# One TensorE visit for states @ w1, attention's small tiles gathered into two slots of three, and batch 0's states doubled on the chip

## The chip, the cores and the metric

The kernel runs on one core of a Trainium2 chip. The time is the device time of one execution in microseconds; before the change it was 436.61 us, the median of three runs (436.3 to 436.9). The profile is one execution of 436.56 us, of which 434.8 us lie between the first and the last instruction; its TensorE clock was granted in full. PE is TensorE, DVE is VectorE, ACT is ScalarE, POOL is GpSimd, SP is the engine that issues most transfers.

## What is computed

Two stages follow each other: a cross attention between tokens and states of each batch and head, and a layer of eight experts in which every row goes to the expert with the largest gate.

```python
# x: (8, 8, 512, 64), state: (8, 8, 32, 64), all fp32
scores = 0.125 * x @ state.T            # per batch b and head h
a      = softmax(scores);   xread = a @ state      # 512 rows
scores2 = 0.125 * state @ x.T
a2     = softmax(scores2);  sread = a2 @ x         # 32 rows
rows   = concat([xread, sread]) -> (8 * 544, 512)  # heads side by side
e      = argmax(rows @ w_gate);  g = max of softmax
out    = g * (relu(rows @ w1[e]) @ w2[e])          # w1: (8, 512, 1024), w2: (8, 1024, 512)
```

The kernel uses two properties of this. All 512 token rows of a batch mostly go to one expert, so a batch is a dense product with that expert's weights; the few others would be repaired behind a branch, which isn't taken with these inputs. And since xread = a @ state, the product xread @ w1 can be taken as a @ (state @ w1): the kernel first forms G = state @ w1 for the batch, from 32 rows per head, and then multiplies the attention weights by G. The 256 state rows are sorted by expert and done in rounds of 128 rows between the batches.

## The kernel before

Work is written as Python generators. `down` and `up` issue the large products of the experts, and after every four large matmul instructions, a "slot", they call `next(insert)`, which issues a step of other work: first the attention of later batches (each batch is a generator `stages(b)`; a new one begins every third slot), then the rounds of the state rows. In the order below the steps of a batch are one slot apart.

```python
def load_states(b, q0, q1):
    rows = state[b].rearrange("h n d -> n h d")
    to = st2[b] = att.tile([64, H, D], FP32, tag="st", bufs=3, name="st2")
    q0.dma_start(out=to[0:32], in_=rows)
    for u in range(2):                     # the same states, halves exchanged
        q1.dma_start(out=to[32:64, :, ts(u, 32)], in_=rows[:, :, ts(1 - u, 32)])

def turn_states(b, copy):                  # stT: transposed by DVE, then copied to the other 64 partitions
    ...
    dve.transpose(to[0:64], st2[b][:].rearrange("p h d -> p (h d)"))
    copy(to[64:128], to[0:64])
    for g in range(2):
        gp.tensor_copy(out=stG[ts(g, 64), b], in_=...)

def stages(b):
    xt, sx = new_xt(b), new_sx()
    for k in range(2):
        turn_x(b, xt, k)                   # DVE: x transposed
    turn_states(b, gp.tensor_copy)
    yield
    states_gates(b)                        # PE pg   64*32 tiles
    pc = new_pc()
    scores(b, xt, pc, 0)                   # PE pc   32*32 tiles
    yield
    scores(b, xt, pc, 1)                   # PE pc
    for i in range(4):
        turn_scores(pc, sx, i)             # DVE sx <- pc
    less_max(sx, ALL, gp)                  # DVE mx, POOL sx
    nm = write_max(pc)                     # DVE nm
    yield
    soft[b] = (sx,) + write_weights(pc, nm)   # ACT a
    exponential(sx, ALL)                   # ACT sx
    over_sum(sx, ALL, gp)                  # DVE sm, POOL sx
    yield
    turn_read(b)                           # DVE aT
    yield
    turn_write(b)                          # PE pt   whole array
    yield
    write_rows(b)                          # PE pw   128*32 tiles
    exps, gates = logits_x(b)              # PE pl   128*32 tiles, then DVE routing
    yield
    exps()
    xsT = turn_rows(b)                     # PE pxs  whole array
    yield
    choose(b)                              # PE pr   whole array
    logits_s(b, [xsT])                     # PE pls  128*32 tiles, DVE lgs
    gates()

def states_w1(G, w1t, st, halves=(0, 1), bank=bank, cut=1):
    for k in halves:
        pg = [bank("pG") for _ in range(2)]
        for q in range(4):
            for g in range(2):             # PE pG  64*32 tiles
                pe.matmul(pg[g][ts(q, 32), :], lhsT=st[ts(g, 64), q, :],
                          rhs=w1t[ts(g, 64), q, ts(k, 512)], start=True, stop=True, ...)
        for c in range(cut):
            for g in range(2):
                act.copy(G[:, g, ...], pg[g][...])
    return G

def between_products(n):                   # after the n-th product pX, pD, pX, pY, pZ, pW of batches 2 to 7
    nonlocal G
    if n in (3, 4) and b + 1 < B:          # one half of G in each of two slots
        if n == 3:
            G = new_G()
        states_w1(G, w1s[b + 1], stG[:, b + 1], (n - 3,), <banks of a second pool>)
    yield
    if n == 4 and b + 2 < B:
        lazy.extend(w1_parts(b + 2, expert_of(eb, b + 2)))
    if n == 5 and b + 1 < B:
        sums_of[b + 1] = up_sums(G, aT[b + 1])
    yield
```

All PSUM tiles that `bank()` gives (pg, pt, pw, pl, pls, pr, pxs, pG, py, ph) share four buffers of one bank each. [...] A matmul of fp32 stands in the profile as two records.

Of the kernel before, what the change touches and what calls it, by code (L numbers as in the profile page):

```python
# [9 lines left out]
FP32 = mybir.dt.float32  # L10
# [10 lines left out]
def kernel(  # L21
# [76 lines left out]

    st2 = {}

    def load_states(b, q0, q1):

        rows = state[b].rearrange("h n d -> n h d")
        to = st2[b] = att.tile([64, H, D], FP32, tag="st", bufs=3, name="st2")
        q0.dma_start(out=to[0:32], in_=rows)
        for u in range(2):
            q1.dma_start(out=to[32:64, :, ts(u, 32)], in_=rows[:, :, ts(1 - u, 32)])

    wg = const.tile([128, NDC, E], FP32)
    wg4 = att.tile([128, NDC, 32], FP32, name="wg4")  # L110
    act.dma_start(out=wg4[:, :, 0:E], in_=moe_w_gate.rearrange("(p c) e -> p c e", c=NDC))
    load_states(0, sp, act)
    load_x(0, sp)
    dve.memset(wg4[:, :, E:], 0.0)
    warm = const.tile([128, 1], FP32)
# [74 lines left out]
    blank = ffn.tile([128, XW], I32, tag="y", bufs=YB, name="blank")  # L190
    gp.memset(blank[:], 0)
    gp.memset(blank[:, DM + 1:DM + 2], FAR)
    gp.memset(gst[:], 0.0)

    soft, rows_of = {}, {}
# [12 lines left out]
    def turn_states(b, copy):  # L208

        stT[b] = att.tile([128, H, 2, NS], FP32, tag="stT", bufs=2, name="stT")  # L210
        to = stT[b][:].rearrange("p h u n -> p (h u n)")
# [3 lines that stand above are left out]
            gp.tensor_copy(out=stG[ts(g, 64), b], in_=stT[b][:].rearrange("p (q g) u n -> p g u q n", g=2)[ts(g, 64), g, 0])  # L215
# [61 lines left out]
    def new_xt(b):  # L277

        return [(att, ffn)[b % 2].tile([128, 4, NC, 2, 32], FP32, tag=("xt0", "xt1", "Sa", "Sb")[2 * (b % 2) + k], name="xt")
                for k in range(2)]  # L280

    def new_sx():
        return att.tile([128, 4, NB, NS], FP32, tag="sx", bufs=2, name="sx")
# [35 lines left out]
    def fetch_batch(b):  # L319
        if b < B:  # L320
            load_x(b, sp)
            load_states(b, sp, sp)

    def turn_read(b, i=ALL):
        if b not in aT:
            aT[b] = att.tile([128, 4, 2, 128], FP32, tag="aT", bufs=NE, name="aTe")[:]
        dve.transpose(aT[b][:, i].rearrange("p i g s -> p (i g s)"),
                      soft[b][0][:, i].rearrange("p i b n -> p (i b n)"))
        if i.stop == 4 and b != 1:
            keep_read(b)  # L330
# [14 lines left out]
    def stages(b):  # L345

        xt, sx = new_xt(b), new_sx()
        for k in range(2):
            turn_x(b, xt, k)
        turn_states(b, gp.tensor_copy)  # L350
        yield
        states_gates(b)
        pc = new_pc()
        scores(b, xt, pc, 0)
        yield
        scores(b, xt, pc, 1)
        for i in range(4):
            turn_scores(pc, sx, i)
        less_max(sx, ALL, gp)
        nm = write_max(pc)  # L360
        yield
        soft[b] = (sx,) + write_weights(pc, nm)
        exponential(sx, ALL)
        over_sum(sx, ALL, gp)
        yield
        turn_read(b)
        yield
        turn_write(b)
        yield
        write_rows(b)  # L370
        exps, gates = logits_x(b)
        yield
        exps()
        xsT = turn_rows(b)
        yield
        choose(b)
        logits_s(b, [xsT])
        gates()

    def turn_rows(b):  # L380

# [42 lines left out]
    def choose(b):  # L424

        most(b, count(b))
# [17 lines left out]
    def begin():  # L444
# [17 lines left out]
        most(0, pr)  # L462
        keep_warm(6)
        xt, sx = new_xt(0), new_sx()
        turn_x(0, xt, 0)
        turn_states(0, act.copy)
        e = expert_of(eb, 0)
        at_once(w1_parts(0, e, 2))
        load_x(1, sp)
        load_states(1, sp, sp)  # L470
        sp.dma_start(out=wg[:], in_=moe_w_gate.rearrange("(c p) e -> p c e", p=128))
        at_once(w2_parts(0, e))
        fetch_batch(2)
# [33 lines left out]
        up(G, aT[0], hT, two, fs=far)  # L507
        nm = write_max(pc)
        xt, sx = new_xt(1), new_sx()
        for k in range(2):  # L510
            turn_x(1, xt, k)
        turn_states(1, gp.tensor_copy)
        first_e = att.tile([1, 1], FP32, name="first_e")
        dve.tensor_copy(out=first_e[:], in_=eb[0:1, 0:1])

# [71 lines left out]
    def new_G():  # L587
        return ffn.tile([128, 2, F], FP32, tag="G", name="G")

    def states_w1(G, w1t, st, halves=(0, 1), bank=bank, cut=1):  # L590

        for k in halves:
            pg = [bank("pG") for _ in range(2)]
# [3 lines that stand above are left out]
                              rhs=w1t[ts(g, 64), q, ts(k, 512)], start=True, stop=True, skip_group_check=True)  # L597
            for c in range(cut):
                for g in range(2):
                    act.copy(G[:, g, ts(cut * k + c, 512 // cut)], pg[g][:, ts(c, 512 // cut)])  # L600
        return G

    def new_hT():
# [107 lines left out]
        next(insert, None)  # L711
        return hT

    def down(hT, w2t, store, insert=None, between=None):
        for c in range(NC):
            py = bank("py")
            for f in range(NFC):
                pe.matmul(py[:], lhsT=hT[f // 2][:, f % 2, ts(c, 128)], rhs=w2t[:, f, :],
                          start=(f == 0), stop=(f == NFC - 1))
                if insert and f == 3:  # L720
                    next(insert, None)
            store(c, py)
            if insert:
                step = between(c)
                next(step)
                next(insert, None)
                next(step)
# [340 lines left out]
    def first():  # L1068

        write_rows(0)  # L1070
        keep_read(1)
        yield
        turn_write(1)
        yield
        exps, gates = logits_x(1)
        yield
        exps()
        choose(1)
        e1 = expert_of(eb, 1)
        at_once(w1_parts(1, e1))  # L1080
        lazy.extend(w2_parts(1, e1))
        gates()
        count(0)
        yield
        write_rows(1)
        yield
        xsT = [turn_rows(b) for b in range(2)]
        yield
        logits_s(0, xsT)
# [8 lines left out]
    def attention():  # L1098

        gens, slot = [first()], 0  # L1100
        while gens:
            b = 2 + slot // 3
            old, new = gens[:], slot % 3 == 0 and b < B
            begun = slot < 6
            if slot == 2:
                early.append(stages(3))
                next(early[0])
            if begun:
                advance(gens, old[:1])
            if new:  # L1110
                if not early:
                    early.append(stages(b))
                    next(early[0])
                gens.append(early.pop())
            advance(gens, old[1:] if begun else old)
            slot += 1
            yield

# [8 lines left out]
    def batch(b):  # L1127

        nonlocal G, hT

        def between(c):
            nonlocal G
            if c == 1 and b:
                G = states_w1(new_G(), w1s[b + 1], stG[:, b + 1])
            yield
            if c == 2 and not b:
                G = states_w1(new_G(), w1s[b + 1], stG[:, b + 1])
            if c == 1 and 0 < b < B - 2:
                lazy.extend(w1_parts(b + 2, expert_of(eb, b + 2)))
            yield  # L1140

        def between_products(n):
            nonlocal G
            if n in (3, 4) and b + 1 < B:
                if n == 3:
                    G = new_G()
                states_w1(G, w1s[b + 1], stG[:, b + 1], (n - 3,),
                          lambda name: late["ps_t"].tile([128, 512], FP32, tag="t", bufs=2, name=name))
            yield
            if n == 4 and b + 2 < B:  # L1150
                lazy.extend(w1_parts(b + 2, expert_of(eb, b + 2)))
            if n == 5 and b + 1 < B:
                sums_of[b + 1] = up_sums(G, aT[b + 1])
            yield

        if b < NE:
            down(hT, w2s[b], store_batch(b), slots, between)
        else:
            last = down_by_halves(b, hT, w2s[b], slots, between_products)
        if 0 < b < B - 2:  # L1160
            lazy.extend(w2_parts(b + 2, expert_of(eb, b + 2)))
        if b + 1 in sums_of:
            hT = up_by_halves(G, aT[b + 1], sums_of[b + 1], new_hT(), slots)
        elif b + 1 < B:
            hT = up(G, aT[b + 1], new_hT(), insert=slots, at=(1, 3, 5, 7) if b + 1 < NE else (1, 3, 4, 5, 6, 7))
        if b == B - 1:
            return last
        if b == 0:
            e2 = expert_of(eb, 2)
            lazy.extend(w1_parts(2, e2) + w2_parts(2, e2))  # L1170
# [130 lines left out]
```

## Time and profile before

| | busy, us | share of the 434.8 us span | instructions |
|---|---|---|---|
| PE | 425.4 | 98% | 3925 |
| PE weight loads | 287.9 | 66% | 3925 |
| DVE | 220.6 | 51% | 475 |
| POOL | 153.7 | 35% | 144 |
| ACT | 128.9 | 30% | 297 |

| part of the work, all batches | records | busy, us |
|---|---|---|
| pG (states @ w1), 64*32 tiles | 256 | 17.1 |
| pc (scores), 32*32 tiles | 1024 | 19.1 |
| pw (a2 @ x), 128*32 tiles | 512 | 8.9 |
| pl, pls (gates of rows), 128*32 tiles | 192 | 8.2 |
| pg (gates of states), 64*32 tiles | 128 | 2.5 |
| pt, pxs (transposes), whole array | 72 | 10.8 |

A group is named "out<-in" by the tiles that it writes and reads; "128*32" is the part of the array that one matmul takes, in rows and columns, and "x32" the number of records. In a timeline the columns are the start, the time from the first start to the last end, the engine, the line (48, the recording helper, for nearly all), the operation, the tiles, the shape and, in brackets, how long the engine was idle before and for whom it waited. Matmuls overlap, so what one of them costs the stream is read from the difference of two starts. 110 MB are moved by DMA at a mean of 253 GB/s.

### The profile page before, as it was taken

To read this page: it belongs to the slowest core of one execution; us is meant where nothing else is said; L and a number is where in the kernel's file an instruction comes from. 1 tells how busy PE (TensorE), PEld (TensorE's weight loads), DVE (VectorE), ACT (ScalarE), POOL (GpSimd) and SP (SyncE) were. 2 spreads that over 40 slices of the span, in tenths; PEclk is the share of its full clock that TensorE was granted. 3 is DMA by queue.
4 is the path that set the end of the run, shared out by engine and by line. 5 is a ranking of instruction groups with operands and counts; after the bars stand their busy time and mean duration, and the time that the engine had idled before them with its cause. 6 is when DMAs were issued, how large, how long until landed. Compare 5 with 4: busy or idle time off the path is not lost.

```text
span 434.8 us, 10177 instructions
## 1 busy us (share of the span) xinstructions
PE 425.4 (98%) x3925; PEld 287.9 (66%) x3925; DVE 220.6 (51%) x475; ACT 128.9 (30%) x297; POOL 153.7 (35%) x144
## 2 busy tenths in 40 slices
PE   6899999999999999999999999999999999999996
PEld 5686555555545558786668667776867685768665
DVE  5658967587686557333415261624442370527142
ACT  1455133552452532212321241013240242015100
POOL 2010231223222512473427424634336253644231
PEclk9999999999999999999999999999999999999999
DMA  7990659664685454899999699689948998975212
GB/s 218 319 326 4 190 176 328 200 217 134 201 310 171 134 201 133 309 349 404 386 390 354 200 331 392 258 281 396 384 150 236 402 386 279 311 247 214 97 35 74
DMA packets 64899, 110.06 MB, mean 253 GB/s; under 512 B 13327, under 2 KB 22799, under 8 KB 64848
## 3 DMA queue, kind: packets, MB, share of 16 engines
q1 hardware_dynamic: 60240, 99.99, 66.6%
q0 software_dynamic: 2240, 7.08, 4.3%
q10 hardware_dynamic: 2368, 2.31, 1.5%
q8 instruction: 32, 0.52, 0.5%
q14 instruction: 19, 0.16, 0.1%
HBM read 94.15 MB, written 14.95 MB: 251 GB/s over the span
## 4 chain that ended last, share of the span: by engine, by line
PE 94%; DVE 2%; DMA 1%; ACT 0%; issue 0%; ACTq 0%; POOL 0%; DVEq 0%
PE ph L48 23%; PE py L48 13%; PE pX L48 10%; PE pD L48 8%; PE pY L48 5%; PE pZ L48 5%; PE pgy L48 5%; PE pgh L48 5%; PE pW L48 5%; PE pc L48 4%; PE pG L48 3%; PE pw L48 2%; PE pt L48 2%; PE pE L48 2%; DMA st<-in_state_dram 1%; PE pl L48 1%
## 5 line engine op out<-in xcount | busy, mean ns | idle before, releaser
L48 PE MATMUL py<-w2t,hT 128*128 128x512 f32 x128 | 59.1, 604 | 0.0
L48 DVE TENSOR_TENSOR hT<-ph,hT 128x512 f32<-128x512 f32 x50 | 34.6, 692 | 40.7 <-PE ph L48 40.7
L48 POOL TENSOR_TENSOR Ta<-w2t,Ta 128x1024 f32<-128x1024 f32 x12 | 30.6, 2546 | 46.6 <-PE pY L48 19.9
L48 PE MATMUL pX<-w2t,hT 128*128 128x256 f32 x192 | 43.7, 381 | 0.0
L48 PEld LDWEIGHTS pX<-w2t,hT 128*128 128x128 f32 x192 | 36.2, 190 | 6.4 <-issue 1.7
L48 PEld LDWEIGHTS py<-w2t,hT 128*128 128x128 f32 x128 | 23.0, 189 | 26.3 <-issue 25.3
L48 ACT ACTIVATE hT<-ph 128x512 f32<-128x512 f32 (+2 forms) x50 | 22.7, 462 | 40.2 <-PE ph L48 40.2
L48 PE MATMUL ph<-aTl,G 128*128 128x256 f32 (+1 forms) x112 | 33.8, 444 | 0.0
L48 PE MATMUL ph<-aTe,G 128*128 128x128 f32 (+2 forms) x128 | 30.4, 388 | 1.6 <-DVE aTe L48 1.4
L48 DVE SCALAR_TENSOR_TENSOR yh<-pY,gw,yh 128x256 f32<-128x256 f32 x22 | 9.2, 477 | 44.3 <-PE pY L48 37.7
L48 ACT ACTIVATE yh<-pX,gw 128x256 f32<-128x256 f32 x34 | 13.7, 474 | 52.6 <-PE pX L48 52.6
L48 POOL DMA_DIRECT2D out_dram<-yh x23 | 16.8, 730 | 34.3 <-DVE yh L48 17.6
L48 ACT ACTIVATE hT<-hT 128x512 f32<-128x512 f32 x30 | 18.9, 630 | 30.7 <-DVE hT L48 30.7
L48 PEld LDWEIGHTS ph<-aTl,G 128*128 128x128 f32 x112 | 20.6, 190 | 9.6 <-issue 7.7
L48 PEld LDWEIGHTS ph<-aTe,G 128*128 128x128 f32 x128 | 18.8, 191 | 10.3 <-issue 6.5
L48 POOL TENSOR_TENSOR sx<-sx,mx 128x1024 f32<-128x1024 f32 x6 | 11.5, 1912 | 38.4 <-DVE mx L48 38.4
L48 ACT COPY G<-pG 128x512 f32<-128x512 f32 (+1 forms) x34 | 17.1, 567 | 23.9 <-PE pG L48 23.9
L48 PE MATMUL pY<-Ta,Sa 128*128 128x256 f32 x96 | 22.2, 384 | 0.0
L48 ACT COPY hT<-ph 128x512 f32<-128x512 f32 x10 | 5.9, 586 | 55.1 <-issue 43.1
L48 PE MATMUL pZ<-Tb,Sb 128*128 128x256 f32 x96 | 22.1, 383 | 0.0
L48 PEld LDWEIGHTS pY<-Ta,Sa 128*128 128x128 f32 x96 | 17.8, 190 | 6.4 <-issue 3.4
L48 POOL TENSOR_TENSOR Tb<-w2t 128x1024 f32<-128x1024 f32 x6 | 14.2, 2369 | 22.2 <-issue 22.2
(187 smaller groups left out, 736.2 us busy)
## 6 DMA issues: line engine op xcount, KB each, us to landing
s<-in_moe_w_dram SPq DMA_DIRECT2D x192, 256.0 KB, 5.8
w2t<-in_moe_w_dram SPq DMA_DIRECT2D x32, 512.0 KB, 6.8
w1t<-in_moe_w_dram SPq DMA_DIRECT2D x28, 512.0 KB, 7.4
x_nat<-in_x_dram SPq DMA_DIRECT2D x16, 512.0 KB, 4.9
out_dram<-yh POOLq DMA_DIRECT2D x23, 256.0 KB, 4.5
at_dram<-aTl SPq DMA_DIRECT2D x6, 512.0 KB, 6.2
w1t<-in_moe_w_dram SPq DMA_DIRECT2D x2, 1024.0 KB, 4.9
out_dram<-y ACTq DMA_DIRECT2D x8, 256.0 KB, 5.5
```

The source lines that it names most:

```text
L48: ins = getattr(self.engine, name)(*args, **kw)
```

## The change

It has four parts. G of the next batch, from batch 2 on, is computed in one slot rather than two halves in two slots, at a product chosen for each batch (`at`), and its results are copied out by ACT and DVE in turn; for batches 0 and 1 the same product moves by a slot or two. The steps of a batch's attention are arranged anew, so that in every third slot TensorE has only whole-array work (pr, pxs) and the steps with small tiles stand side by side in the other two, while the small vector work of the routing is spread over them. The second copy of batch 0's states is made by GpSimd from the first rather than loaded by two more transfers. And states are transposed before x rather than after it.

```diff
-    def load_states(b, q0, q1):
+    def load_states(b):
...
-        q0.dma_start(out=to[0:32], in_=rows)
-        for u in range(2):
-            q1.dma_start(out=to[32:64, :, ts(u, 32)], in_=rows[:, :, ts(1 - u, 32)])
+        sp.dma_start(out=to[0:32], in_=rows)
+        if b:
+            for u in range(2):
+                sp.dma_start(out=to[32:64, :, ts(u, 32)], in_=rows[:, :, ts(1 - u, 32)])
...
     gp.memset(blank[:, DM + 1:DM + 2], FAR)
+
+    for u in range(2):
+        gp.tensor_copy(out=st2[0][32:64, :, ts(u, 32)], in_=st2[0][0:32, :, ts(1 - u, 32)])
     gp.memset(gst[:], 0.0)
...
     def stages(b):
         xt, sx = new_xt(b), new_sx()
+        turn_states(b, gp.tensor_copy)
         for k in range(2):
             turn_x(b, xt, k)
-        turn_states(b, gp.tensor_copy)
         yield
...
+        turn_write(b)
         turn_read(b)
-        yield
-        turn_write(b)
         yield
         write_rows(b)
         exps, gates = logits_x(b)
         yield
         exps()
+        choose(b)
         xsT = turn_rows(b)
         yield
-        choose(b)
+        gates()
+        yield
         logits_s(b, [xsT])
-        gates()
...                                         # batch 0
+        turn_states(0, act.copy)
         turn_x(0, xt, 0)
-        turn_states(0, act.copy)
...                                         # batch 1
+        turn_states(1, gp.tensor_copy)
         for k in range(2):
             turn_x(1, xt, k)
-        turn_states(1, gp.tensor_copy)
...                                         # states_w1: copies by act.copy, or by evict (ACT and DVE in turn)
-                    act.copy(G[:, g, ...], pg[g][...])
+                    (copy or act.copy)(G[:, g, ...], pg[g][...])
...                                         # down: a call before the slot that stands inside a product
                 if insert and f == 3:
+                    if ahead:
+                        ahead(c)
                     next(insert, None)
...                                         # first(): batch 1's last steps
-        yield
         write_rows(1)
+        yield
         yield
...                                         # attention(): order of the generators in a slot
+            fresh = []
+            if (slot == 2 or slot % 3 == 0 and b < B) and not early:
+                early.append(stages(3 if slot == 2 else b))
+                next(early[0])
+            if slot % 3 == 0 and b < B:
+                fresh = [early.pop()]
+            advance(gens, gens[-1:] + gens[:-1] if slot % 3 == 1 and slot > 1 else gens[:])
+            gens += fresh
...                                         # batches 0 and 1
-            if c == 1 and b:
+            if c == 2 and b:
                 G = states_w1(new_G(), w1s[b + 1], stG[:, b + 1])
...
+        def ahead(c):
+            nonlocal G
+            if c == 3 and not b:
+                G = states_w1(new_G(), w1s[b + 1], stG[:, b + 1])
...                                         # batches 2 to 6
+        at = {3: 2, 4: 1, 5: 5}.get(b, 3)
         def between_products(n):
             nonlocal G
-            if n in (3, 4) and b + 1 < B:
-                if n == 3:
-                    G = new_G()
-                states_w1(G, w1s[b + 1], stG[:, b + 1], (n - 3,), <banks of a second pool>)
+            if n == at and b + 1 < B:
+                G = states_w1(new_G(), w1s[b + 1], stG[:, b + 1], (0,), late_bank, copy=evict)
+                states_w1(G, w1s[b + 1], stG[:, b + 1], (1,), copy=evict)
             yield
-            if n == 4 and b + 2 < B:
+            if n == at and b + 2 < B:
                 lazy.extend(w1_parts(b + 2, expert_of(eb, b + 2)))
```

More of the change, by code (lines that the diff above doesn't have):

```diff
@@ L111 @@
     act.dma_start(out=wg4[:, :, 0:E], in_=moe_w_gate.rearrange("(p c) e -> p c e", c=NDC))
-    load_states(0, sp, act)
+    load_states(0)
     load_x(0, sp)
@@ L321, in fetch_batch @@
             load_x(b, sp)
-            load_states(b, sp, sp)
+            load_states(b)
     def turn_read(b, i=ALL):
@@ L469, in begin @@
         load_x(1, sp)
-        load_states(1, sp, sp)
+        load_states(1)
         sp.dma_start(out=wg[:], in_=moe_w_gate.rearrange("(c p) e -> p c e", p=128))
@@ L588, in new_G, with states_w1 @@
         return ffn.tile([128, 2, F], FP32, tag="G", name="G")
-    def states_w1(G, w1t, st, halves=(0, 1), bank=bank, cut=1):
+    def states_w1(G, w1t, st, halves=(0, 1), bank=bank, cut=1, copy=None):
         for k in halves:
@@ L599, in states_w1 @@
                 for g in range(2):
-                    act.copy(G[:, g, ts(cut * k + c, 512 // cut)], pg[g][:, ts(c, 512 // cut)])
+                    (copy or act.copy)(G[:, g, ts(cut * k + c, 512 // cut)], pg[g][:, ts(c, 512 // cut)])
         return G
@@ L712, in up_by_halves, with down @@
         return hT
-    def down(hT, w2t, store, insert=None, between=None):
+    def down(hT, w2t, store, insert=None, between=None, ahead=None):
         for c in range(NC):
@@ L1083, in first @@
         count(0)
+        write_rows(1)
         yield
-        write_rows(1)
         yield
@@ L1102, in attention @@
             b = 2 + slot // 3
[L1103 to L1106, printed above, removed]
+            fresh = []
+            if (slot == 2 or slot % 3 == 0 and b < B) and not early:
+                early.append(stages(3 if slot == 2 else b))
                 next(early[0])
[L1108 to L1115, printed above, removed]
+            if slot % 3 == 0 and b < B:
+                fresh = [early.pop()]
+            advance(gens, gens[-1:] + gens[:-1] if slot % 3 == 1 and slot > 1 else gens[:])
+            gens += fresh
             slot += 1
@@ L1132, in between, with late_bank @@
             nonlocal G
-            if c == 1 and b:
+            if c == 2 and b:
                 G = states_w1(new_G(), w1s[b + 1], stG[:, b + 1])
             yield
-            if c == 2 and not b:
-                G = states_w1(new_G(), w1s[b + 1], stG[:, b + 1])
-            if c == 1 and 0 < b < B - 2:
+            if c == 2 and 0 < b < B - 2:
                 lazy.extend(w1_parts(b + 2, expert_of(eb, b + 2)))
             yield
+        at = {3: 2, 4: 1, 5: 5}.get(b, 3)
+        def late_bank(name):
+            return late["ps_t"].tile([128, 512], FP32, tag="t", bufs=2, name=name)
+        def ahead(c):
+            nonlocal G
+            if c == 3 and not b:
+                G = states_w1(new_G(), w1s[b + 1], stG[:, b + 1])
         def between_products(n):
             nonlocal G
-            if n in (3, 4) and b + 1 < B:
-                if n == 3:
-                    G = new_G()
-                states_w1(G, w1s[b + 1], stG[:, b + 1], (n - 3,),
-                          lambda name: late["ps_t"].tile([128, 512], FP32, tag="t", bufs=2, name=name))
+            if n == at and b + 1 < B:
+                G = states_w1(new_G(), w1s[b + 1], stG[:, b + 1], (0,), late_bank, copy=evict)
+                states_w1(G, w1s[b + 1], stG[:, b + 1], (1,), copy=evict)
             yield
-            if n == 4 and b + 2 < B:
+            if n == at and b + 2 < B:
                 lazy.extend(w1_parts(b + 2, expert_of(eb, b + 2)))
@@ L1156, in batch @@
         if b < NE:
-            down(hT, w2s[b], store_batch(b), slots, between)
+            down(hT, w2s[b], store_batch(b), slots, between, ahead)
         else:
```

## Prediction

> **What bounds the kernel now.** I read the page first, then TensorE's own waits, then the timeline.
>
> ```profile
> PE 425.4 (98%) x3925; PEld 287.9 (66%) x3925; DVE 220.6 (51%) x475; ACT 128.9 (30%) x297; POOL 153.7 (35%) x144
> ...
> PE 94%; DVE 2%; DMA 1%; ACT 0%; issue 0%; ACTq 0%; POOL 0%; DVEq 0%
> ```
>
> The first line is busy time, the second the shares of the chain that ended last: TensorE carries 94% of it. Its waits view adds up to 5.4 us, all before 31 us. So after 31 us only a shorter TensorE stream can shorten the span, and in the first 31 us DVE and two transfers count too. The stream holds the same products before and after, so I ask what they cost beyond their steady pace. The timeline of TensorE in batch 2's second layer (start us, us, operation):
>
> ```profile
> 171.16 3.62 PE L48 MATMUL pX<-w2t,hT 128*128 128x256 f32 x16
> 174.71 1.09 PE L48 MATMUL pG<-w1t,stG 64*32 64x512 f32 x16
> 175.73 3.72 PE L48 MATMUL pY<-Ta,Sa 128*128 128x256 f32 x16
> 179.38 1.09 PE L48 MATMUL pG<-w1t,stG 64*32 64x512 f32 x16
> 180.40 3.72 PE L48 MATMUL pZ<-Tb,Sb 128*128 128x256 f32 x16
> 183.96 3.62 PE L48 MATMUL pW<-Ta,hT 128*128 128x256 f32 x16
> 187.41 3.62 PE L48 MATMUL pD<-w2t,Sa 128*128 128x256 f32 x16
> ```
>
> Take differences of starts, since the durations overlap. pW to pD, between two products that use the whole array, is 3.45. pX, followed by pG on 64*32 tiles, takes 174.71 - 171.16 = 3.55. pY, between two pGs, takes 3.65. So a product pays 0.10 when another tile shape follows and 0.10 when one stood before. pG itself is 1.02 for 16 records; batch 1's pG, with 32 records in one piece, takes 1.88 (69.08 to 70.96). Sixteen records are therefore 0.86, and 0.16 is paid per visit. A visit changes the tile shape twice and costs 0.10 + 0.16 + 0.10 = 0.36: **0.18 us per change of shape**. It buys nothing.
>
> The head, where TensorE is not the limit:
>
> ```profile
> 4.70 2.93 PE L48 MATMUL idle<-ident 128*128 128x128 f32 x12
> 5.31 0.15 DVE L48 TENSOR_REDUCE eb<-c_cc 1x1 int32<-1x8 f32 x1
> 6.10 1.25 DVE L48 STREAM_TRANSPOSE xt<-x_nat 128x1024 f32<-128x1024 f32 x1 [0.64 <-DMA x_nat<-in_x_dram]
> ...
> 7.96 0.70 DVE L48 STREAM_TRANSPOSE stT<-st 64x512 f32<-64x512 f32 x1 [0.61 <-DMA st<-in_state_dram]
> ...
> 8.69 0.62 ACT L48 COPY stT<-stT 64x512 f32<-64x512 f32 x1 [4.51 <-DVE stT L48]
> ```
>
> DVE waits until 7.96 for the second copy of batch 0's states; ACT's copy of the transpose ends at 9.31; the scores pc run in earnest from 9.36 to about 12.8, and the chain of waits goes on from there through DVE.
>
> **What the Trainium skill says.** "TensorEngine Tiling", section Tiling Modes (Key Properties): changing the tiling mode, not just the tile, drains TensorE. The trace agrees, at 0.18 us per change. "TensorE: Matmul & The Clock Gate", Part 1: the array runs at half clock until it has been busy for about a 3.4 us window, and falls back when idle. The trace agrees in kind: 12 idle matmuls from 4.70 took 2.93 us, 10 from 13.94 took 1.38. "DMA: Bandwidth & Descriptors", Rules for kernel authors: under 64 KB a transfer is mostly overhead. The two 32 KB state loads took 5.6 us to landing, the 512 KB loads of x 4.9. "Perfetto Trace Analysis", Identifying the Most-Contended Engine: busy matmul time says little of headroom; the 98% here indeed hides the changes of shape.
>
> **The change, part by part.**
>
> *1. States @ w1 in one slot (batches 2 to 6).* Two visits of 16 records become one of 32, in batches 3, 4 and 5 beside a small-token product (128*32 tiles) that already broke the stream. In the built programs' TensorE order the changes of shape go 4 to 2, 6 to 3, 6 to 3, 6 to 3 and 5 to 3: 13 fewer.
>
> *2. Attention in two slots of three.* A steady period before is nine changes: into pw/pl and out; into pg, to pc, out; into pls, out to pt, into pc, out. After, one slot has only whole-array work (pr, pxs); the others run pg, pc, then pt and pls, pw, pl, pc: six changes. The period, 91.10 (pw) to 107.21 (next pw) = 16.11, should fall by 3 x 0.18 = 0.54. Over all batches the order shows 12 fewer.
>
> Together 119 become 94, so 25 x 0.18 = **-4.5 us**, all on the path, since TensorE never waits there.
>
> *3. Batch 0's states doubled on chip.* Two loads go, two GpSimd copies of 32x256 come. GpSimd copies 64x128 in 0.28 and 64x512 in 0.61, so I put 0.4 on each: done near 3.8 us (the memset before them ends at 2.92). The transpose of the states now precedes that of x: DVE ends eb at 5.46, transposes states until about 6.2, then x until about 7.4 (0.66 and 1.25 from the rows above). ACT's copy ends at 6.85, hidden beside x. pc then starts when the idle matmuls end, about 7.55 instead of 9.36: **-1.8 us**, passed on by the DVE chain. I also expect TensorE, now without the gap from 7.6 to 9.4, to reach full clock inside pc; half of pc's 3.4 us at double speed would be 0.9, and as I don't know where the clock turns I count **-0.5**. The first half of w1 (issued 6.19; w1's shortest landing is 3.4, so about 9.6) is in time for pG near 10.5.
>
> *4. States before x for batch 1.* Before, pg waited for GpSimd's copy at 30.06 (0.25 us) and pc began at 30.25. After, x's transposes end about 29.4 and pc begins when the product before ends and pg is through, about 29.8: **-0.4 us**.
>
> *5. What it adds.* Every period piles DVE work behind one pc: the routing after pl (1.5), then the chain sx, mx, nm, states, x (69.20 to 75.83 in the trace = 6.6 us). In batch 1's third slot the order now is pc, half a py (3.6), pG (1.9), pls (0.3), pr, and pr must wait until DVE has emptied pls's bank, which stands behind that chain: 0.6 + 6.6 + 0.2 = 7.4 us after pc, when TensorE is there at 5.8. (pG's second half also waits for ACT to empty a bank of the first, inside the same delay.) **+1.7 us**, once.
>
> Sum: -4.5 - 1.8 - 0.5 - 0.4 + 1.7 = -5.5, so 436.6 - 5.5 = **431.1 us**.
>
> **Rivals.** *A: the vector chain becomes the bound of every period.* DVE has about 13 us of work (the chain 6.6, routing 1.5, sums 1.8, read transposes 1.3, small ones 1.8) in a period that shrinks to 15.6. The third slot's pc ends about 12.3 into a period; the vector chain behind it ends 0.6 + 6.6 later, at 19.5, which is 3.9 into the next period. There TensorE wants x's transposes at 4.05 and, at 5.05, pr's bank, which DVE frees 0.7 after its chain, at 4.6. Slacks of 0.15 and 0.45 us; if I am 0.5 off, each of five periods loses that, 2.5 us in all, and most of part 2 is gone: 434. Against it: before the change DVE idled over 2 us at a time in each period (2.12 before the read transposes at 83.16 and 99.72). *B: a change of shape costs less between two array shapes, or where the stream breaks for pgh and pgy anyway.* Then a third of the 4.5 fails: about 432.6. For it: I measured only changes from and to the whole array well; against it: pG before pw takes 1.88 as before py. *C: a transfer sets the start.* If x or w1 lands late, part 3 gives only about 1: 432. *D: weights late.* Batch 4's pG comes two products earlier; but its w1 parts were issued at 229.56 and land in 7 to 9 us, and pG will be near 253, so the transfer stays hidden; batch 6's parts still go out before the block of loads at 344. *E, the good side:* the clock turns early in pc and the slot of part 5 does not stall: 428.5.
>
> **Range and chances.** Rivals A and C together give about 434.2; E gives 428.5; I take 428.6 to 434.0. Over 2% faster needs 427.9 or less, more than E alone: 0.06. Slower by over 2% needs a wait of over 14 us that nothing here shows: 0.02. Within 2%: 0.92.
>
> **What would show it.** Right: pG as one group of 32 records of about 1.9 us in each of batches 2 to 6 and the product after it 3.55; an attention period near 15.5; pc begun near 7.5 and sx's first transpose near 10.5 instead of 12.89; one wait of TensorE for DVE's lgs of about 1 us. Wrong: TensorE waiting in every attention period for xt, cnt or c_cc on DVE, or for hT or y on ACT (rival A); product starts still 3.65 apart (B); DVE still waiting for x or TensorE for w1 near 7 to 11 us (C). A stall I did not place, of several us, in the first 60 us or at a weight load would break the range.

## The result, and the profile after

The changed kernel takes **431.65 us** (median of four executions, 430.85 to 432.29) against 436.58 for the kernel before beside it. The ratio is 0.989, with a 95% interval of 0.987 to 0.990. The prediction was 431.1, and 428.6 to 434.0.

The page of the changed kernel, the same two lines as before, busy time and the chain that ended last:

```profile
PE 420.3 (98%) x3925; PEld 287.4 (67%) x3925; DVE 230.8 (54%) x485; ACT 124.7 (29%) x287; POOL 154.6 (36%) x146
...
PE 90%; DVE 4%; ACT 2%; DMA 1%; POOL 1%; issue 0%; SPq 0%; POOLq 0%; DVEq 0%
```

TensorE is busy 5.1 us less with the same 3925 records: the same matmuls stand closer together, and those of batch 0's scores ran faster (see the head below). Its share of the chain falls from 94% to 90%, though it does not wait longer in sum: the waits below add up to 5.0 us, against 5.4 before. The chain is followed back to whatever released TensorE, so even a wait of 0.2 us brings the work of another engine into it. TensorE's waits view of the changed kernel:

```profile
PE pG L48 <- DMA w1t<-in_moe_w_dram: 1.7, 1, 1.7
PE idle L48 <- POOL ident masks.py:199: 1.5, 1, 1.5
PE prg L48 <- DVE sums L48: 0.8, 1, 0.8
PE ph L48 <- DVE lgs L48: 0.3, 1, 0.3
PE pss L48 <- POOL blank L48: 0.3, 1, 0.3
PE pr L48 <- DVE lgs L48: 0.2, 1, 0.2
PE pg L48 <- ACT hT L48: 0.2, 1, 0.2
```

The waits of ph for aTe (1.4), of pc for stT (1.1) and of pg for stT (0.3) are gone. Four are new: one for a transfer of w1 in the head, and three of 0.2 to 0.3 in the attention. The head, from the timelines of TensorE and DVE:

```profile
4.72 2.93 PE L48 MATMUL idle<-ident 128*128 128x128 f32 x12
5.42 0.70 DVE L48 STREAM_TRANSPOSE stT<-st 64x512 f32<-64x512 f32 x1
6.05 2.32 DVE L48 STREAM_TRANSPOSE xt<-x_nat 128x1024 f32<-128x1024 f32 x2
7.58 2.33 PE L48 MATMUL pc<-xt,stT 32*32 32x128 f32 x128
9.95 0.45 DVE L48 STREAM_TRANSPOSE sx<-pc 128x256 f32<-128x256 f32 x1 [1.58 <-PE pc L48]
11.64 1.22 PE L48 MATMUL pG<-w1t,stG 64*32 64x512 f32 x16 [1.73 <-DMA w1t<-in_moe_w_dram]
14.00 1.95 PE L48 MATMUL ph<-aTe,G 128*128 128x128 f32 x16
16.90 7.69 PE L48 MATMUL ph<-aTe,G 128*128 128x128 f32 x56
```

DVE no longer waits for a second load: it goes from eb straight to the states and then to x. pc starts at 7.58, where the idle matmuls end, and sx is transposed at 9.95 instead of 12.89. The last line is the second call of ph, at 16.90; before, it started at 19.82. TensorE in batch 2's second layer:

```profile
168.09 3.62 PE L48 MATMUL pX<-w2t,hT 128*128 128x256 f32 x16
171.64 1.95 PE L48 MATMUL pG<-w1t,stG 64*32 64x512 f32 x32
173.52 3.72 PE L48 MATMUL pY<-Ta,Sa 128*128 128x256 f32 x16
177.07 3.62 PE L48 MATMUL pZ<-Tb,Sb 128*128 128x256 f32 x16
180.53 3.62 PE L48 MATMUL pW<-Ta,hT 128*128 128x256 f32 x16
```

There is one visit of 32 records, 1.88 from start to start (171.64 to 173.52). The product before it and the one after it take 3.55 each, and none takes 3.65.

The span divides at two records that every kernel has: the first py (batch 0's down product) and the first pX (the late phase). Starts are in us, from the timelines:

| stretch | before | after | difference |
|---|---|---|---|
| head: first py | 37.91 | 34.70 | -3.21 |
| attention: first py to first pX | 126.26 | 126.40 | +0.14 |
| late: first pX to last pE | 263.20 | 260.86 | -2.34 |
| last pE starts | 427.37 | 421.96 | -5.41 |

So part 2, the rearranged attention, gained nothing in the profiled execution. Everything came from the head and the late part. The table flatters the change a little: the profiled execution of the changed kernel is the fastest of its four (430.85 us, 0.8 below their median). The experiments ask why.

### The profile page after: what moved, and what is told of

Read it like the earlier page. It is cut to its first block, busy times and chain, and to the rows that moved or that the text cites. A ratio compares the mean times of both kernels' runs of the same rounds, so it can differ in the third digit from the quotient of the medians.

```text
span 429.0 us, 10186 instructions
## 1 busy us (share of the span) xinstructions
PE 420.3 (98%) x3925; PEld 287.4 (67%) x3925; DVE 230.8 (54%) x485; ACT 124.7 (29%) x287; POOL 154.6 (36%) x146
## 4 chain that ended last, share of the span: by engine, by line
PE 90%; DVE 4%; ACT 2%; DMA 1%; POOL 1%; issue 0%; SPq 0%; POOLq 0%; DVEq 0%
PE ph L48 23%; PE py L48 11%; PE pX L48 10%; PE pD L48 8%; PE pgh L48 5%; PE pgy L48 5%; PE pW L48 5%; PE pY L48 5%; PE pZ L48 5%; PE pG L48 3%; PE pc L48 3%; PE pw L48 2%; PE pt L48 2%; PE pE L48 2%; DMA w1t<-in_moe_w_dram 1%; PE pl L48 1%
## 5 line engine op out<-in xcount | busy, mean ns | idle before, releaser
L48 PE MATMUL pW<-Ta,hT 128*128 128x256 f32 x96 | 21.9, 381 | 0.0
L48 PE MATMUL pgh<-s,sxT 128*32 128x512 f32 x192 | 21.8, 595 | 0.0
L48 PE MATMUL pgy<-s,shT 128*32 128x512 f32 x192 | 21.8, 595 | 0.0
```

Of the source, the lines that this page charges most:

```text
L48: ins = getattr(self.engine, name)(*args, **kw)
```

## The experiments

They ran on three chips: e1 to e4 on one, the control run of the changed kernel, e6, e7 and e8 on a second, and e5, e9, e10 and e12 on a third. Which chip gave the result above ("first chip" below) is not on record. The kernel before took 435.68 us on the first of the three (36 executions), 436.22 on the second (12) and 436.14 on the third (19). These 67 executions lie between 434.8 and 437.2, and the four beside the result all in the upper part of that, 436.3 to 436.9. A ratio is to the kernel before on the same chip. "Outside" is the time less the span, that is, what lies before the first recorded instruction or after the last.

| kernel | median us | ratio to before (95% interval) | pc ends | first py | attention | late | outside |
|---|---|---|---|---|---|---|---|
| before (first chip) | 436.58 | | 12.85 | 37.91 | 126.26 | 263.20 | 1.8 |
| after (first chip) | 431.65 | 0.989 (0.987 to 0.990) | 9.91 | 34.70 | 126.40 | 260.86 | 1.8 |
| e1: part 1 alone | 435.56 | 1.001 (0.999 to 1.002) | 11.12 | 36.18 | 126.25 | 260.86 | 4.0 to 4.6 |
| e2: parts 3 and 4 alone | 434.10 | 0.996 (0.995 to 0.998) | 11.37 | 36.13 | 126.78 | 263.20 | 1.8 |
| e3: part 2 alone | 436.24 | 1.000 (0.999 to 1.002) | 11.88 | 36.93 | 126.49 | 263.20 | 1.8 |
| e4: four visits by records | 447.79 | 1.027 (1.024 to 1.030) | 13.10 | 38.15 | 126.25 | 274.33 | 1.8 |
| e5: four visits by columns | 439.07 | 1.008 (1.006 to 1.010) | 11.95 | 37.00 | 126.26 | 266.33 | 1.8 |
| the changed kernel again | 432.15 | 0.992 (0.989 to 0.995) | 10.78 | 35.66 | 126.62 | 260.85 | 1.8 |
| e6: batch 0's pG moved back | 430.93 | 0.989 (0.986 to 0.992) | 10.53 | 35.50 | 125.22 | 260.85 | 1.8 |
| e7: changed, old head | 436.39 | 1.002 (1.000 to 1.004) | 11.54 | 36.59 | 126.41 | 260.85 | 4.3 to 4.7 |
| e8: warm earlier | 431.53 | 0.990 (0.988 to 0.993) | 10.23 | 35.38 | 126.42 | 260.85 | 1.8 |
| e9: changed, old attention | 432.08 | 0.991 (0.989 to 0.993) | 11.45 | 36.23 | 126.27 | 260.85 | 1.8 |
| e10: e6 and e8 together | 430.30 | 0.987 (0.985 to 0.989) | 11.21 | 35.94 | 125.38 | 260.86 | 1.8 |
| e12: e1 and ten fillers | 436.26 | 1.001 (0.999 to 1.002) | 12.11 | 37.17 | 126.27 | 260.86 | 4.1 to 4.7 |

The stretches are of one profiled execution each. The late stretch comes out the same to 0.01 us wherever its code is the same. The head varies by over 1 us with the execution, so heads are compared with care.

### What a change of tile shape costs: e1, e4, e5

e1 is the kernel before with the change's `between_products` and `at` (the one-slot G and its copies) and nothing else.

> The kernel before with part 1 alone: G of batches 3 to 7 in one visit at the product chosen in the change, copied by ACT and DVE in turn. The built order has 13 fewer changes of shape and nothing else on TensorE. Theory (each change of shape costs the stream about 0.18 us, wherever it stands): 13 x 0.18 = 2.3 us less, 434.2; in the trace, from the first pX of batch 2 to the last pE 2.5 us less than before, no new wait. Rival (the changes are free beside the pgh and pgy products, which break the stream anyway): only batches 2 and 6 save, 4 changes, 0.7 us, 435.9.

Its late stretch is 260.86, or 2.34 shorter than before: 13 changes of shape less (the traces count 43 before and 30 in e1), at 0.18 each. Its time did not fall at all, which is taken up at e12.

e4 goes the other way and spreads the same product over four visits of 8 records:

```diff
-            if n in (3, 4) and b + 1 < B:        # two visits: all four column groups, 512 columns of w1
+            if n in (2, 3, 4, 5) and b + 1 < B:  # four visits: two column groups q, 512 columns of w1
+                for q in ((0, 1) if first else (2, 3)): ...
```

> The opposite of part 1: the kernel before with G of batches 3 to 7 in four visits of 8 records, after the 2nd, 3rd, 4th and 5th product. 18 more changes of shape in the built order, the same records. Theory: 18 x 0.18 = 3.2 us more, 439.8; each visit of 8 records takes 0.43 + 0.16 = 0.59 from its first start to the next product's. Rival (the cost is of the wait for PSUM banks between the halves of G, not of the change of shape): no more than 1 us more, 437.5.

It came out 12 us slower, four times what was expected. The timeline of TensorE in e4, batch 2's second layer:

```profile
171.49 1.06 PE L48 MATMUL pG<-w1t,stG 64*32 64x512 f32 x8
172.48 3.72 PE L48 MATMUL pX<-w2t,hT 128*128 128x256 f32 x16
176.13 1.06 PE L48 MATMUL pG<-w1t,stG 64*32 64x512 f32 x8
177.12 3.72 PE L48 MATMUL pY<-Ta,Sa 128*128 128x256 f32 x16
```

A visit of 8 records takes 0.99 from start to start, and one of 16 took 1.02. "TensorEngine Tiling (Array Packing)", section Tiling Modes (Key Properties), in the Trainium skill, says that different tiles work independently and in parallel. Here that means that leaving out two of the four column groups halves the records and saves no time. The experiment had doubled the work, not only the visits. Twenty visits of 0.99 + 0.20 in place of ten of 1.02 + 0.20 make +11.6, and the late stretch grew by 11.13.

e5 mends it: each visit takes all four column groups, on 256 columns of w1.

```diff
-                for q in ((0, 1) if first else (2, 3)): ... rhs=w1t[..., q, ts(kk, 512)]
+                for q in range(4): ...            rhs=w1t[..., q, ds(512 * kk + 256 * (v % 2), 256)]
```

> The kernel before with the late states @ w1 again in four visits per batch, after products 2 to 5, but each visit now does all four column groups of the array on 256 of the 1024 columns of w1, so that every visit is half a visit of before in time. (In the experiment with four visits of 8 records each visit took 0.99 us from start to start, as much as one of 16 records, 1.02: with half of the array's tiles idle the matmuls were not fewer in a row.) Theory, 0.18 us per change of shape: 18 more changes than before, 18 x 0.18 = +3.2, so 438.9 to 439.5 if before is 435.7 to 436.2; each visit about 0.59 from start to start and the product between two visits 3.65. Rival: the extra 12 us of the earlier experiment came from something else that four visits bring (waits for banks, copies on ScalarE); then it stays far above, at 443 or more.

```profile
170.34 0.66 PE L48 MATMUL pG<-w1t,stG 64*32 64x256 f32 x16
170.94 3.72 PE L48 MATMUL pX<-w2t,hT 128*128 128x256 f32 x16
174.59 0.66 PE L48 MATMUL pG<-w1t,stG 64*32 64x256 f32 x16
175.18 3.72 PE L48 MATMUL pY<-Ta,Sa 128*128 128x256 f32 x16
```

Visits are 0.59 and 0.60 from start to start, and the product between two of them takes 3.65, as worked out. The late stretch is 266.33, which is 3.13 over before for 18 more changes (61 in the trace), or 0.174 each. Fewer changes (e1) and more changes (e5) give the same price, and the rival of other waits is out.

### What the rearranged attention brings: e3, e9, e6

e3 is the kernel before with part 2 alone (`stages`, `first`, `attention`, and batch 0's and 1's G where the change has them).

> The kernel before with part 2 alone: the attention's steps rearranged, and G of batches 1 and 2 moved with them; the head and the late batches as before. 12 fewer changes of shape, worth 2.2 us, against waits for PSUM banks that the trace of the changed kernel shows at four places (about 2.3 us). Theory: they cancel, 436.4 to 436.8, with the waits of pG, pr, pg and ph in the trace again. Rival (the waits come from the shortened head, which brings the vector engines' work nearer): no waits here, 434.4.

e9 is the other half of the test, the changed kernel without part 2.

> The changed kernel with the attention of the kernel before (its slots, and batch 0's states @ w1 in its old place), so parts 1, 3 and 4 without part 2. Theory: part 2 brings 0.54 per clean period but its stalls (pG's bank and pr in batch 1's third slot, pg for ScalarE, ph for lgs) take back about as much, so this kernel is where the changed kernel is or up to 0.5 below: 431.6 to 432.2, if the changed kernel is 432.15 as its control run said. Rival: part 2 brings its 12 changes x 0.18 = 2.2 less 1.7; then this kernel is 0.5 slower than the changed one, 432.6.

Both agree that part 2 is worth nothing as it stands: 436.24 against 435.68 for e3 (ratio 1.000), and 432.08 for e9 against 432.15 with part 2, though these two ran on different chips (ratios to before 0.991 and 0.992). The attention stretch is 126.4 to 126.6 with part 2 in five kernels (126.49 in e3) and 126.25 to 126.27 without it in six of seven (126.78 in e2, where one pc of 64 records took 1.52 instead of 1.00, with nothing in the trace that it waited for). Yet the clean period is shorter: in the changed kernel pr starts at 106.15 and again at 121.82, a period of 15.67 against 16.11. The saving is given back in single stalls. They are not owed to the new head: e3, which has the old one, waits at pr, pg and ph as the changed kernel does. The largest is in batch 1's third slot. TensorE there, in the changed kernel:

```profile
67.05 3.70 PE L48 MATMUL py<-w2t,hT 128*128 128x512 f32 x8
70.68 2.93 PE L48 MATMUL pG<-w1t,stG 64*32 64x512 f32 x32
73.54 0.57 PE L48 MATMUL pls<-wg,xsT 128*32 128x8 f32 x16
74.36 0.24 PE L48 MATMUL pr<-oh,ones_b 128*128 128x8 bf16 x4 [0.25 <-DVE lgs L48]
```

pG takes 2.86 (70.68 to 73.54) where it takes 1.88 everywhere else, and no idle time is put before it because the wait is inside the group. It needs four banks of a pool of four while py is half done and holds one. The view by tile shows the wait at its weight loads, 0.9 us for ACT's copy of G, which empties a bank of the first half. Then pr waits for DVE to empty the bank of pls. e6 puts batch 0's G back between two products:

```diff
             yield
+            if c == 2 and not b:
+                G = states_w1(new_G(), w1s[b + 1], stG[:, b + 1])
...
-        def ahead(c):
-            if c == 3 and not b: ...
```

> The changed kernel with batch 0's call of states @ w1 (32 records for batch 1) moved back to where the kernel before had it, after the third down product and its slot, when no accumulation py holds a bank. Theory: pG took 2.86 us at 70.68 instead of 1.88 because its fourth bank was not free while py held one; that goes, and so does most of the 0.48 that pr waited for lgs; one more change of shape comes (pG no longer stands beside pls): -1.0 - 0.3 + 0.2 = -1.1 against the changed kernel, about 430.1 if that is 431.2. Rival: the slot is set by the vector chain behind pc (pls's bank is emptied by DVE only after it), so TensorE waits the same time at pr, and the time stays within 0.3.

```profile
67.85 1.95 PE L48 MATMUL pG<-w1t,stG 64*32 64x512 f32 x32
69.73 3.70 PE L48 MATMUL py<-w2t,hT 128*128 128x512 f32 x8
73.36 0.57 PE L48 MATMUL pls<-wg,xsT 128*32 128x8 f32 x16
73.87 0.25 PE L48 MATMUL pr<-oh,ones_b 128*128 128x8 bf16 x4
```

pG is back at 1.88, pr follows pls without a wait (0.51 from start to start, 0.82 in the changed kernel), and the time falls by 1.2 to 430.93 (430.5 to 431.0, against 432.0 to 432.3 on the same chip). The one more change of shape that was expected isn't there: the trace counts 48 in the attention stretch with and without the edit. DVE's chain is as long as before, and copies lgs only at 74.96, 1.1 us after pr has started. So the chain held this slot only because no other bank was free. With e6 the attention stretch is 125.22 (125.38 in e10), so 0.9 to 1.0 shorter than before the change, and part 2 earns something.

### What the head brings: e2, e7, e8

e2 is the kernel before with the states doubled on GpSimd and, for batches 0 and 1, the states transposed ahead of x.

> The kernel before with parts 3 and 4 alone: batch 0's second copy of the states made by GpSimd, states transposed before x for batches 0 and 1. Theory (the scores start when the states are there, and the clock turns to full because TensorE has no gap from 7.6 to 9.4): pc of batch 0 from 7.6 to 9.9 rather than 9.36 to 12.8, first py near 34.7 rather than 37.9, 3.2 us less in all, 433.4. Rival (the loads saved are what counts, the order and the clock are not): 1.8 us less, 434.8, with pc still 3.4 us long.

It gives 1.6 us, less than the 2.7 of the prediction's parts 3 and 4, and less than the 3.21 between the first chip's two profiles. Two reasons can be read. First, in the experiments the gate's weights land later, in 3.0 to 3.3 us (the eleven profiles that list it) against 2.3 in the first chip's two profiles. DVE's transpose of them, in the changed kernel on the first chip and then in its control run here:

```profile
3.15 0.31 DVE L48 STREAM_TRANSPOSE wgT<-wg 128x128 f32<-128x128 f32 x1
```

```profile
3.82 0.31 DVE L48 STREAM_TRANSPOSE wgT<-wg 128x128 f32<-128x128 f32 x1 [0.60 <-DMA wg<-in_moe_w_gate_dram]
```

The idle matmuls then end later and pc starts at 8.1 to 8.5 with the new head, not at 7.58. The old head loses nothing by it, since it waits for the second load of the states anyway: the bulk of its pc starts at 9.13 in e1 and at 9.36 in the first chip's profile. Second, the length of pc differs between executions: 2.33 in the changed kernel, 2.65 in its control, 3.01 in e2, 2.21 in e6 and 3.21 in e9, all with the same head. The durations of single records point to TensorE's clock. The pc records of before, of after and of e1, from the view by tile (duration in ns, shortest/median/longest):

```profile
L48 PE MATMUL pc<-xt,stT x128: 367/416/418, 8.7 to 12.4; 32*32 32x128 f32 x128
```

```profile
L48 PE MATMUL pc<-xt,stT x128: 267/268/418, 7.6 to 9.6; 32*32 32x128 f32 x128
```

```profile
L48 PE MATMUL pc<-xt,stT x128: 267/268/292, 8.5 to 10.9; 32*32 32x128 f32 x128
```

Before, all ran slow (median 416 ns). After, most ran fast (268), and the first ones did not. In e1, with the old head, all ran fast. The granted clock that the profile lists is 1.00 in these stretches of all three, so the turn is read from the durations alone. The Trainium skill, "TensorE: Matmul & The Clock Gate", Part 1, says that the window over which TensorE's activity is judged runs freely and is not tied to the kernel's start. The runs agree: the turn falls at another point of pc in each execution. It is not tied to the new head either: e1 with the old head (all fast) and e2 with the new one (median 416) reach the first py within 0.05 us of each other, at 36.18 and 36.13. So the 1.2 us by which pc became shorter between the first chip's two profiles is luck of two executions and not shown to be a gain of the change.

e7 is the changed kernel with the old head, parts 1 and 2 alone.

> The changed kernel with the head of the kernel before (its own two loads for the second copy of the states, x before the states), so parts 1 and 2 alone. If the parts add, it is the kernel before less 2.3 (part 1 as the trace of the first experiment showed it: its late part was 2.3 shorter) plus or minus 0.5 for part 2: 433.4 to 433.9 against 435.7, ratio about 0.995. If part 1 is worth nothing in time, as its own run said (435.6, with a span that was 2.5 shorter and 2.3 us outside the span), it is 435.7 again, and the difference between the time and the span is again 4.1 instead of 1.8.

Its median span is 431.9, between before (434.45) and the changed kernel (430.3), so by spans the head is worth 1.6 here as in e2. Its time is that of before, because its time outside the span is again above 4. e8 fills the gap between pss and prg with two more idle matmuls, four records:

```diff
                       start=True, stop=True, skip_group_check=True)   # pss
+        keep_warm(2)
```

> The changed kernel with four more matmuls on the identity right after pss, in TensorE's gap before prg (3.65 to 4.45). Theory: the clock of TensorE turned full only inside pc because of the gaps before it; with the gap filled it turns earlier and pc's 128 matmuls take 2.0 us rather than 2.3 to 3.0: -0.3 to -1.0 at the end of pc and the same in time (430.2 to 430.9 if the changed kernel is 431.2). Rival: the clock turns at moments that do not depend on how the stream before was filled; then pc takes anything from 2.0 to 3.4 and the time stays or rises by 0.2, as prg comes a little later.

It took 0.6 less than the control (431.45 to 431.93 against 431.97 to 432.34), and pc took 2.03, fast from its first record. But in e10, with the same edit, the profiled pc took 2.73. So the edit does not fix the moment of the turn, as the rival said. That it shortens the time rests on four executions of each kernel, which do not overlap; how it would do so is open.

The same table answers the rival of the control run:

> The changed kernel itself, as a control beside the three others. The chip of the first four experiments showed the kernel before at 435.7, 0.9 below the first chip, so the changed kernel should stand near 431.2, a ratio of 0.989 as before. Theory: the second product ph starts 7.0 us after the scores pc end, in every kernel so far, so a head that ends pc near 9.9 or 10.5 gives all of the head's gain, and TensorE's wait for w1 ahead of pG costs nothing. Rival: the wait of 1.7 us for w1 is paid in full; then a run in which w1 lands later has a second ph later than 7.0 us after pc.

The second call of ph starts 6.96 to 7.01 after pc's end wherever TensorE's wait for w1 was 1.1 us or less (eleven profiles: 19.82 - 12.85 before, 17.75 - 10.78 in the control). With waits of 1.7 to 1.9 it is 6.99 (after), 7.18 (e6) and 7.36 (e8). What follows pc is DVE's softmax chain. TensorE waits for w1 beside it, at a cost of nothing up to 1.1 us and of 0.4 at most beyond.

### Time outside the span: e12

e1, e7 and then e12 showed over 4.0 us outside the span in every execution, all others 1.7 to 1.9. e12 adds instructions to e1 to see if the length of an engine's program decides:

```diff
     act.activation(warm[:], warm[:], AF.Exp)
+    for _ in range(10):
+        act.activation(warm[:], warm[:], AF.Exp, scale=-1.0)
```

> The first experiment (part 1 alone) with ten tiny activations of a 128x1 tile more on ScalarE, at its start where it has nothing to do. Part 1 alone had a span 2.5 us shorter than before, but 4.1 us of its time lay outside the span instead of 1.8, and so did parts 1 and 2 together (4.3 to 4.7), each in every execution, and in no other kernel. Theory: what lies outside hangs on how many instructions an engine has, not on what part 1 does; then with ten more on ScalarE (part 1 took ten from it) it returns to 1.8 and the time falls to 433.3. Rival: it belongs to part 1 with the old head itself; then it stays at 4.1, 435.6.

It stayed, at 4.1 to 4.7. The three kernels are those that combine part 1 with the old head. The page shows one other thing that is theirs alone, the packets of the second instruction queue: 17, 17 and 18, where all others have 19 or 20. Of e1 and of the changed kernel:

```profile
q14 instruction: 17, 0.14, 0.1%
```

```profile
q14 instruction: 19, 0.16, 0.1%
```

Nothing here shows that one has to do with the other, and the cause stays open. For the accounts it means that part 1's 2.3 us is real in the span and, in these runs, reaches the time only together with the new head: e9 (parts 1, 3 and 4) is 4.06 below before, while e1 gave -0.1 and e2 -1.6.

### Both edits: e10

> The changed kernel with both of the edits that helped: batch 0's states @ w1 back after the third down product's slot (-1.2 in its run) and the four earlier idle matmuls (-0.6). If they add, 432.15 - 1.8 = 430.3, a ratio of 0.987 to before. Rival: with pc hot in any case and w1 landing near 12.0, the head is now bounded by w1, so the second gives only part: 430.6.

430.30 us (430.1 to 431.1), against 432.15 for the changed kernel in its control run on another chip. The median is where it should be if the two edits add, but the five executions also hold the rival's 430.6 and overlap those of e6 alone (430.5 to 431.0), so that they add is not shown. This version beats both the kernel before and the changed kernel.

## Why the prediction was right, and where it was not

The total of -5.5 met a measured -4.9 on the first chip and -4.1 in the control run on another. That it came so near is in part luck: part 2 with its stalls was put at -0.5 (-2.2 + 1.7) and came to +0.1, and the head was put at -2.7 and came to -3.2, by a turn of the clock that belongs to the pair of executions. Two small slips of its sums change nothing: 7.4 less 5.8 is 1.6, not 1.7 (part 5), and rivals A and C together (2.5 and 0.8 more than 431.1) give 434.4, not 434.2; both lie above the upper end of its range. Its steps, against the first chip's traces:

- **0.18 us per change of shape: right.** The late part's 13 changes gave 2.34 (2.34 by the rule), and e5's 18 in the other direction cost 3.13. Rival B is out: products are 3.55 apart, not 3.65.
- **Part 2, 12 changes less (-2.2): right in kind, lost in the sum.** A clean period came to 15.67 (-0.44, predicted -0.54). The stretch as a whole grew by 0.14. With the 2.14 of stalls in the next point, the twelve changes saved 2.0, or 0.17 each.
- **Part 5, +1.7 in one slot: near in size, wrong order of causes.** 1.29 was lost there, 0.98 in pG and 0.31 at pr (0.82 from pls to pr against 0.51 in e6). The prediction put it on pr behind the vector chain and took pG's bank as hidden inside that. The bank came first and was the larger, and e6 removed both by freeing it. What it did not place was 0.85 more: pg waits for ACT's hT at 94 us (0.45 lost against a clean slot) and ph waits until 149.78 for lgs (0.40). That is rival A, in one of five periods and once besides, not in each.
- **Part 3, pc's start (-1.8): right on the first chip** (9.36 to 7.58). **The clock (-0.5): its reason was wrong.** pc in earnest took 3.5 before and 2.33 after, so -1.2. The prediction put it down to the gap from 7.6 to 9.4 that goes, but without the gap pc took anything from 2.21 (e6) to 3.21 (e9, most records slow), and in e1, where the old head leaves a smaller gap, 124 records took 1.99, all fast. The term depends on the execution and can have either sign.
- **w1 "in time" near 9.6: wrong**, it came at 11.64. Rival C's wait appeared, 1.7 us long, but cost next to nothing: the second ph started 6.99 us after pc's end, against 6.97 before.
- **Part 4 (-0.4): right.** Second ph to batch 1's pc: 10.43 before, 10.15 after, so -0.3.
- **Rival D (weights late): did not happen.** TensorE has no wait for a weight after the head.

## What to carry to other kernels

Price a change of tile shape from the starts of one stream (here 0.17 to 0.18 us) and multiply by the count in the built order. It held within 4% in both directions in the late stretch, where TensorE never waits; in a clean period of the attention three changes brought 0.15 each, and single stalls took the sum back. Before moving a group into the middle of an accumulation, count the PSUM banks that it and the open group need together: the wait shows as a longer group, not as idle time. In a head of a few microseconds, judge edits by repeated executions, because the clock's turn and the first transfers move it by as much as the edit does.

## What the runs showed of the hardware that was not expected

- pG by 8 records on half of the column groups takes as long as by 16 on all (0.99 against 1.02 us).
- TensorE's clock turned at a different point of the same pc in each execution: 2.21 to 3.21 us for the same 128 records in the five profiles with the change's head as it stands, and fast throughout (1.99 for 124 records) in one with the old head.
- In three kernels 4.0 to 4.7 us of the time lay outside the span instead of 1.8, for a reason that stayed open.
